# One written order for a kernel's opening: ten attention units, 32 weight pieces and 22 feed-forward steps

## The chip, the core and the metric

The kernel runs on one core of a Trainium2 chip. TensorE (PE) multiplies matrices, and its weight loads run beside its products; VectorE (DVE), ScalarE (ACT) and GpSimd (POOL) work element by element; SyncE (SP) here issues DMA transfers. Each engine takes its own instructions in their order and waits for the others by semaphores. The metric is the device time of one execution in microseconds (us); lower is better.

## The reference

Three stages follow each other: attention over a causal window of 64 keys, a dense feed-forward layer, and a layer of eight experts of which each token uses one. Reshapes and loops are cut.

```python
# q, k, v: (4, 8, 576, 64)
rel = pos[:, None] - pos[None, :]
mask = (rel >= 0) & (rel < 64)
scores = np.where(mask, np.matmul(q, k.T) / 8, -1e9)
attn = softmax(scores)
x = np.matmul(attn, v)                 # -> (2304 tokens, 512)

h = x @ w_in                           # (512, 2048)
g = np.where(h >= 1, h, np.where(h <= -1, 0, (h + 1) ** 2 / 4))
x = g @ w_out                          # (2048, 512) -> (2304, 512)

e = argmax(x @ w_gate)                 # 8 experts
out = gate_w * (np.maximum(x @ w1[e], 0) @ w2[e])
```

## The kernel before

All arithmetic is float32. A factor of a large product is held as a high part in the rounded format that TensorE takes (fp32r) and a low part, what the rounding left; a product is three passes (high with high, low with high, high with low).

**Units.** Attention is cut into 36 units: 128 tokens and four of the eight heads each. A unit (`unit_parts`) goes through: scores on PE with the mask added there (`u_qk`, L308 and L312), a maximum on VectorE (L351, L363), its scaled negative on ScalarE (L372), four exponentials on ScalarE (L382), a sum's reciprocal (L392, L393) and the scaling by it (L396, VectorE for units in `NORM_V`, else GpSimd), a transpose on PE (L420) and its copy on ScalarE (L423), the product with the values on PE (L438), and its split into high part (ScalarE, L450) and low part (VectorE, L452) in `xT`. The data of the first ten units (`qqr`, `vte`) lie in early buffers; units 10 and on load into one buffer for scores (`qk`, `RB = 1`) and one for values (`vt`, `VB = 1`), so that a load waits until the unit ahead has used its own.

**Weight pieces.** `w_in` and `w_out` arrive as doubles, in 16 pieces of 512 KB each (`wi`, `wo`, one for each f). Integer instructions turn a piece into float32 (`split_parts`): one on ScalarE (L193), three on VectorE (L206, L209, L213) or, for seven pieces (`SGN_P`), two on VectorE (L201, L209) beside one on GpSimd (L198); then the high part on ScalarE (L217) and the low part on GpSimd (L219). Two intermediate buffers `t` are shared by all pieces.

**Steps.** The dense layer takes the tokens in seven blocks (0 to 6) of 256 or 384 tokens (`BLOCKS`). A step is one block and one f: twelve matmuls (L482) into `h`, an activation (ScalarE L491, L492, VectorE L494, ScalarE L499 for the high part, L500 for the low part on VectorE or GpSimd by `GLO_P`), and the second layer (L519) into accumulators. `SEG` gives the order of blocks: before, block 0 does steps f = 0 to 7, then block 1 all 16, then block 0 the other eight, then blocks 2 to 6. A block's steps need the units of its tokens: units 0 to 3 for block 0, 4 to 9 for block 1, 10 to 13 for block 2. A second layer runs two steps behind its first.

**What sets the order.** `FIRST` lists the first 28 loads on SP. `HEAD` lists parts of units 0 to 3 and of weight pieces 0 to 4; `in_order` chains what these parts issue, engine by engine, as they are written. After that the units follow a plan of slots (`PLAN`, two slots to a step), the pieces follow due times (`wsplit`), and a scheduler at build time sets the order on PE, VectorE, ScalarE and GpSimd from the traced program. SP keeps the traced order up to step 8 (`SPN`); the loads of units 10 and on are traced between those of pieces.

Of the kernel before, what the change touches and what calls it, by code (L numbers as in the profile page):

```python
# [19 lines left out]
P = 128  # L20
# [14 lines left out]
RATE2 = 2  # L35
LA = 0
SPN = 8
SEG = [(0, 0, 8), (1, 0, 16), (0, 8, 16), (2, 0, 16), (3, 0, 16), (4, 0, 16), (5, 0, 16), (6, 0, 16)]
PLAN = {1: (-2, 16), 2: (36, 60), 3: (56, 84), 4: (86, 116), 5: (124, 150), 6: (154, 178)}
EARLY = 10  # L40
# [14 lines left out]
VB = 1  # L55
SGN_P = (10, 13, 16, 19, 20, 24, 30)
LEAD = (16, 0, 0)
ALT = 4
NQ = 15
MASK_PE = tuple(range(NQ))  # L60
GLO_P = (0, 1, 3, 4, 6, 7)
FIRST = "u0 m c u1 u2 v0 w u3 w v1 v2 w v3 w u4 u5 w v4 u6 v5 w u7 v6 u8 v7 u9 v8 v9".split()
DEPTH = 6, 3


HEAD = (
# [3 lines left out]
).split()  # L70
NORM_V = (0, 1, 2, 3, 12, 14, 32)
NORM_P = 14
# [3 lines left out]
KHI_V = (1, 4, 5, 7, 8, 9, 10, 15, 20, 26, 29, 30, 32, 34, 35)  # L76
PRO_A = 1
PRO_B = 6
WARM = 10
# [25 lines left out]
def mask_constants():  # L105

    r = np.arange(P)
    i = r[:, None] % 64
    ok = (r[None] >= i + 1) & (r[None] <= i + 64)
    new = ok & (r[None] >= 64)  # L110
    up = r[:, None] < 64
    m = np.stack([ok, np.where(up, new, ok), np.where(up, ok, new)], axis=1)
    return np.where(m, 0.0, NEG).astype(np.float32)


@with_exitstack
def kernel(
# [28 lines left out]
    ident = ct[:, C_ID:C_ID + P]  # L146
    mb = att.tile([P, 3, P], BF16, name="mb")
    ib = att.tile([P, P], BF16, name="ib")
    half = cp.tile([P, 1], F32, name="half")
# [23 lines left out]
    def load_w(kind, f):  # L173
        src = wi if kind == "i" else wo
        if f < KF - 2:
            raw = wp.tile([P, 512, 2], I32, tag="w", name="wraw")
        else:
            raw = sp.tile([P, 512, 2], I32, tag="st", name="sraw")
        nc.sync.dma_start(raw, src[:, f].bitcast(I32).rearrange("p (a b) -> p a b", b=2))
        return kind, f, raw  # L180

    def whole(gen):

        def run(*a):
            for _ in gen(*a):
                pass
        return run

    def split_parts(kind, f, raw):
        hw, lw = raw[:, :, 1], raw[:, :, 0]  # L190
        t = att.tile([P, 512], I32, tag="t", name="t", bufs=2)
        w = wp.tile([P, 2, 512], F32R, tag="w", name="w" + kind)
        nc.scalar.activation(t.bitcast(F32), hw.bitcast(F32), ACTF.Abs, scale=2.0**-112)  # L193
        yield
        onpool = 2 * f + (kind == "o") in SGN_P
        if onpool:

            nc.gpsimd.tensor_scalar(  # L198
                out=w[:, 1], in0=hw.bitcast(F32), scalar1=0.0, scalar2=None, op0=ALU.mult
            )  # L200
            nc.vector.scalar_tensor_tensor(  # L201
                out=t, in0=t, scalar=3, in1=w[:, 1].bitcast(I32), op0=ALU.logical_shift_left,
                op1=ALU.bitwise_or,
            )
        else:
            nc.vector.tensor_scalar(  # L206
                out=t, in0=t, scalar1=3, scalar2=None, op0=ALU.logical_shift_left
            )
# [3 lines left out]
        if not onpool:
            nc.vector.scalar_tensor_tensor(  # L213
                out=t, in0=hw, scalar=-0x80000000, in1=t, op0=ALU.bitwise_and, op1=ALU.bitwise_or
            )
        yield
        nc.scalar.activation(w[:, 0], t.bitcast(F32), ACTF.Copy)  # L217
        yield
        nc.gpsimd.tensor_tensor(  # L219
            out=w[:, 1], in0=t.bitcast(F32), in1=w[:, 0].bitcast(F32), op=ALU.subtract  # L220
        )
        (win if kind == "i" else wout)[f] = w

    split_w = whole(split_parts)

# [59 lines left out]
    def u_qk(u):  # L285
# [8 lines left out]
        if u < NQ:  # L294
# [5 lines left out]
            for pr in range(2):  # L300
# [4 lines left out]
                if pe:  # L305
                    for a, r, rows, o in outs:
                        m = 1 + a if kind == 1 + r else 0
                        nc.tensor.matmul(  # L308
                            o, ib[rows, 64 * a:64 * a + 64], mb[rows, m], start=True, stop=False
                        )  # L310
                for a, r, rows, o in outs:
                    nc.tensor.matmul(  # L312
# [175 lines left out]

    def act_g(h, n, pool):
        a = gp.tile([P, NG], F32, tag="a", name="a", bufs=2)  # L490
        nc.scalar.activation(a[:, :n], h[:, :n], ACTF.Relu, scale=0.5, bias=half[:, 0:1])  # L491
        nc.scalar.activation(a[:, :n], a[:, :n], ACTF.Square)  # L492

        nc.vector.scalar_tensor_tensor(  # L494
            out=a[:, :n], in0=h[:, :n], scalar=1.0, in1=a[:, :n], op0=ALU.max, op1=ALU.min
        )
        hi = gp.tile([P, NG], F32R, tag="ghi", name="ghi")
        lo = gp.tile([P, NG], F32R, tag="glo", name="glo")
        nc.scalar.activation(hi[:, :n], a[:, :n], ACTF.Copy)  # L499
        (nc.gpsimd if pool else nc.vector).tensor_tensor(  # L500
            out=lo[:, :n], in0=a[:, :n], in1=hi[:, :n].bitcast(F32), op=ALU.subtract
# [389 lines left out]
    for i, x in enumerate(FIRST):  # L891
        if x == "w":
            wload()
        elif x == "m":
            mt = sp.tile([P, 3, P], F32, tag="st", name="mt")
            nc.sync.dma_start(mt, msk)
            nc.vector.tensor_copy(mb, mt)
        elif x == "c":
            nc.sync.dma_start(ct, cst)
            nc.vector.tensor_copy(ib, ident)  # L900
        else:
# [11 lines left out]
    for j in range(NB2):  # L913
        for f in range(KF2):
            steps.append((2, j, f, f == 0, f == KF2 - 1, False))
    PRO = PRO_A * len(ub_[0]) + PRO_B
    base = PRO
    slots = {}
# [89 lines left out]
    f_at = {}
    for i, (ph, b, f, *_) in enumerate(steps):
        if ph == 1:  # L1010
            f_at.setdefault(f, i)

    def wsplit(s=None):

        if pend:
            kind, f = pend[0][:2]
            due = base + 2 * f_at[f] + (5 if kind == "o" else 0)
            if s is not None and due - s > LEAD[0] + LEAD[1] * f // 16:
                return
            split_w(*pend.pop(0))  # L1020
            if len(pend) < DEPTH[f >= 4]:
                wload()

    def run_slot(s):
# [6 lines left out]

    for _ in range(LA):
        wload()
    def in_order(traced):

        last = {}
        for i in traced:
# [6 lines left out]
            last[i.engine] = i  # L1044

    head = {}
    bb = nc.cur_bb.bb
    seen = {i.name for i in bb.instructions}
    for x in HEAD:
        k = int(x[-1])  # L1050
        key = x[:-1] in ("ab", "s", "hc", "wl"), k
        if key not in head:
            head[key] = split_parts(*pend.pop(0)) if key[0] else unit_parts(k)
        next(head[key], None)
    in_order([
        i for i in bb.instructions if i.name not in seen
        and i.engine in (mybir.EngineType.PE, mybir.EngineType.DVE, mybir.EngineType.Activation, mybir.EngineType.Pool)
    ])
    for _ in range(5):
        wload()  # L1060
    for s in range(PRO):
        run_slot(s)
    acc, g = {}, {}
    for i in range(len(steps) + 2):
        if i == SPN:
            sp_order.close()
        if i < len(steps):
            ph, b, f = steps[i][:3]
            if ph == 1:
                n = blocks[b][1]  # L1070
                while f not in win:
                    wsplit()
                g[i] = act_g(layer1(xT[b], win[f], n), n, i in GLO_P)
            else:
                g[i] = act_relu(layer1(xT2[b], W2["p"][0][f], NG), NG)
        run_slot(base + 2 * i)
        wsplit(base + 2 * i)
        if i >= 2:
            ph, b, f, first, last, partial = steps[i - 2]
            n = blocks[b][1] if ph == 1 else NG  # L1080
            if first:
                acc[ph, b] = accs(n)
            if ph == 1:
                while f not in wout:
                    wsplit()
                w = wout[f]
            else:
                w = W2["p"][1][f]
            layer2(acc[ph, b], g.pop(i - 2), w, first, last)
            if last:  # L1090
                if ph == 1:
                    evac1(b, acc.pop((ph, b)), partial)
                else:
                    evac2(b, acc.pop((ph, b)))
        run_slot(base + 2 * i + 1)
        if i == len(steps) - 1 + LEFT[0]:
            L["h"] = left1(L["w"], L["xl"])
        if i == len(steps) - 1 + LEFT[1]:
            L["g"] = left_turn(L["h"])
        if LEAD[2]:  # L1100
            wsplit(base + 2 * i + 1)

# [71 lines left out]
```

## Time and profile before

| | us |
|---|---|
| median of three runs | 756.37 (756.35 to 757.07) |
| the profiled execution, whole | 757.15 |
| its span, first to last instruction | 755.4 |

| engine | busy us | share of the span |
|---|---|---|
| PE | 719.0 | 95% |
| VectorE | 496.0 | 66% |
| ScalarE | 419.0 | 55% |
| GpSimd | 207.8 | 28% |

The busy time is that of an engine with at least one instruction in work. A view by stretches gives, for windows of the span, the busy time of each engine, the clock granted to TensorE (1.00 is 2.4 GHz, 0.50 is 1.2 GHz), the DMA engines' share and the rate of transfers. A timeline lists instructions with their start and duration and, in brackets, how long the engine had been idle and for whom. On VectorE a following instruction can start a little before the one ahead has ended, so that the distance of two starts is what an instruction takes of the engine. Lines in brackets above are lines of the kernel before.

### The profile page before, as it was taken

The page shows a single profiled execution, that of the slowest core. Times are in us where ns is not written, and L with a number is a line of the kernel's source. Part 1 is how long each engine was busy: PE and PEld are TensorE (multiplying, and loading weights), DVE is VectorE, ACT ScalarE, POOL GpSimd, SP SyncE. Part 2 cuts the span into 40 slices and gives each one's busy share as a digit, 9 for nine tenths or more (in the row PEclk, how much of TensorE's full clock was granted, in tenths as well). Part 3 has the DMA queues.
Part 4 walks back from the last instruction along what each step waited for, and adds up shares of the span by engine and source line. Part 5 has one row for each costly group of instructions (what it writes and reads, how often), then busy time and mean ns, then how long its engine had stood idle before and what let it go on. Part 6 is the DMA issues. An engine that isn't in the chain of part 4 may idle for free. (4 is left out here: it accounts for less than half of the span.)

```text
span 755.4 us, 12426 instructions
## 1 busy us (share of the span) xinstructions
PE 719.0 (95%) x4507; PEld 631.3 (84%) x4507; DVE 496.0 (66%) x1053; ACT 419.0 (55%) x1031; POOL 207.8 (28%) x162
## 2 busy tenths in 40 slices
PE   6597799999999999999999999999999999999996
PEld 3475689888898999888988899987888999888985
DVE  5998988535758655776687334887779989752110
ACT  5777765575757775865586534466443325163212
POOL 0467744202412211330320000366220202065100
PEclk8799899999999999999999999999999999999999
DMA  9940630223432421535254321443334233053101
GB/s 330 402 163 19 208 138 29 57 84 112 154 99 84 143 96 58 173 91 127 62 176 90 83 85 67 123 131 106 117 71 119 49 105 85 23 152 125 44 1 53
DMA packets 66690, 83.77 MB, mean 111 GB/s; under 512 B 35671, under 2 KB 41559, under 8 KB 66498
## 3 DMA queue, kind: packets, MB, share of 16 engines
q1 hardware_dynamic: 66466, 82.52, 35.5%
q8 instruction: 36, 0.59, 0.3%
q0 software_dynamic: 160, 0.43, 0.2%
q14 instruction: 28, 0.23, 0.1%
HBM read 60.74 MB, written 14.42 MB: 100 GB/s over the span
## 5 line engine op out<-in xcount | busy, mean ns | idle before, releaser
L482 PE MATMUL h<-xT,wi 128*128 128x384 f32 (+1 forms) x1344 | 233.4, 321 | 7.4 <-ACT xT L450 3.8
L482 PEld LDWEIGHTS h<-xT,wi 128*128 128x128 f32 x1344 | 212.2, 192 | 20.6 <-DVE a L494 5.4
L519 PE MATMUL acc<-wo,ghi 128*128 128x512 f32 x576 | 155.5, 397 | 0.7 <-ACT wo L217 0.7
L519 PEld LDWEIGHTS acc<-wo,ghi 128*128 128x128 f32 x576 | 103.2, 188 | 16.5 <-ACT wo L217 1.1
L614 DVE CUSTOM_DVE_ANT_0 junk<-xg,wgb 128x512 bf16<-128x512 f32 x144 | 113.8, 790 | 3.2
L482 PE MATMUL h<-xT,we 128*128 128x384 f32 x576 | 110.6, 338 | 3.6 <-DVE glo L509 3.6
L482 PEld LDWEIGHTS h<-xT,we 128*128 128x128 f32 x576 | 101.8, 188 | 9.6 <-DVE glo L509 5.3
L494 DVE SCALAR_TENSOR_TENSOR a<-h,a 128x384 f32<-128x384 f32 (+1 forms) x112 | 55.5, 496 | 63.8 <-ACT a L492 63.2
L500 DVE TENSOR_TENSOR glo<-a,ghi 128x384 fp32r<-128x384 f32 (+1 forms) x106 | 71.4, 674 | 37.7 <-ACT ghi L499 37.6
L519 PE MATMUL acc<-wo,glo 128*128 128x512 f32 x288 | 85.3, 394 | 0.2
L491 ACT ACTIVATE a<-h,half 128x384 f32<-128x384 f32 (+1 forms) x112 | 58.7, 525 | 43.8 <-PE h L482 41.9
L519 PE MATMUL acc<-we,ghi 128*128 128x512 f32 x288 | 78.4, 394 | 0.0
L499 ACT ACTIVATE ghi<-a 128x384 fp32r<-128x384 f32 (+1 forms) x112 | 53.0, 474 | 38.7 <-DVE a L494 38.4
L519 PEld LDWEIGHTS acc<-wo,glo 128*128 128x128 f32 x288 | 53.6, 188 | 13.1 <-POOL glo L500 1.1
L508 ACT ACTIVATE ghi<-h 128x384 fp32r<-128x384 f32 x48 | 23.1, 481 | 71.2 <-PE h L482 62.4
L509 DVE SCALAR_TENSOR_TENSOR glo<-h,ghi 128x384 fp32r<-128x384 f32 x48 | 26.6, 555 | 52.7 <-ACT ghi L508 52.7
L519 PEld LDWEIGHTS acc<-we,ghi 128*128 128x128 f32 x288 | 53.0, 188 | 8.2
L959 POOL TENSOR_TENSOR xT<-xj,xT 128x256 fp32r<-128x256 f32 x36 | 31.4, 883 | 90.4 <-ACT xT L958 90.4
L492 ACT ACTIVATE a<-a 128x384 f32<-128x384 f32 (+1 forms) x112 | 53.1, 475 | 2.3
L282 POOL TENSOR_TENSOR qs<-qk,qs 128x768 fp32r<-128x768 f32 x18 | 34.7, 1926 | 68.0 <-DVE qs L274 27.7
L279 POOL TENSOR_TENSOR qs<-qk,qs 64x512 fp32r<-64x512 f32 x16 | 22.0, 1377 | 109.7 <-ACT qs L272 82.5
L688 POOL TENSOR_TENSOR we<-er,we 128x512 fp32r<-128x512 f32 x16 | 23.9, 1499 | 99.4 <-DMA er<-in_w_dram 87.2
(169 smaller groups left out, 940.6 us busy)
## 6 DMA issues: line engine op xcount, KB each, us to landing
qk<-in_qk_dram SPq DMA_DIRECT2D x21, 640.0 KB, 3.9
er<-in_w_dram SPq DMA_DIRECT2D x32, 256.0 KB, 2.8
wraw<-in_wi_dram SPq DMA_DIRECT2D x14, 512.0 KB, 7.5
wraw<-in_wo_dram SPq DMA_DIRECT2D x14, 512.0 KB, 6.9
vt<-in_vv_dram SPq DMA_DIRECT2D x26, 256.0 KB, 2.8
xg<-x2s SPq DMA_DIRECT2D x18, 256.0 KB, 2.7
out_dram<-y SPq DMA_DIRECT2D x18, 256.0 KB, 2.1
qqr<-in_qq_dram SPq DMA_DIRECT2D x10, 320.0 KB, 7.2
```

The costliest lines, as they stand in the source:

```text
L282: keng.tensor_tensor(out=k, in0=raw[:, 512:], in1=kh.bitcast(F32), op=ALU.subtract)
L482: nc.tensor.matmul(h[:, :n], w[:, wa, k * P:k * P + P], x[:, xa, k, :n], start=(i == 0), stop=(i == 3 * KD - 1),)
L491: nc.scalar.activation(a[:, :n], h[:, :n], ACTF.Relu, scale=0.5, bias=half[:, 0:1])
L492: nc.scalar.activation(a[:, :n], a[:, :n], ACTF.Square)
L494: nc.vector.scalar_tensor_tensor(out=a[:, :n], in0=h[:, :n], scalar=1.0, in1=a[:, :n], op0=ALU.max, op1=ALU.min)
L499: nc.scalar.activation(hi[:, :n], a[:, :n], ACTF.Copy)
L500: (nc.gpsimd if pool else nc.vector).tensor_tensor(out=lo[:, :n], in0=a[:, :n], in1=hi[:, :n].bitcast(F32), op=ALU.subtract)
L509: nc.vector.scalar_tensor_tensor(out=lo[:, :n], in0=h[:, :n], scalar=0.0, in1=hi[:, :n].bitcast(F32), op0=ALU.max, op1=ALU.subtract,)
L519: nc.tensor.matmul(a, ga[:, t * P:t * P + P], w[:, wa], start=(first and j == 0), stop=(last and j == 2),)
L614: tc.keep_in_program_order(nc.vector.tensor_tensor_reduce(out=junk, in0=xg[t], in1=Z["wgb"][:, e], scale=1.0, scalar=0.0, op0=ALU.mult, op ...
L688: nc.gpsimd.tensor_tensor(out=w[:, 1], in0=raw, in1=w[:, 0].bitcast(F32), op=ALU.subtract)
L959: (nc.vector if 2 * t + i in PL_V else nc.gpsimd).tensor_tensor(out=lo, in0=r, in1=hi.bitcast(F32), op=ALU.subtract)
```

## The change

The opening is written out whole. `HEAD` now lists 369 parts: the ten units 0 to 9, all 32 weight pieces, and the parts of 22 steps (`ga` first layer, `rl` the two activations, `st`, `gh`, `gl`, `gb` second layer, `ev` a block's evacuation), and `in_order` chains all that they issue. The steps' function is cut into parts for this (`act_parts`, `step_parts`). Block 0 does six steps first instead of eight. Each piece's part `s` issues the next piece's load, eight pieces ahead; SP keeps the traced order to the end of the chain, and the loads of unit 10 alone are traced inside it.

All 32 low parts of the weights move from GpSimd (L219) to VectorE (L223 of the changed kernel), and the seven pieces of `SGN_P` go the way of the others. Scalings of units 4, 6 and 8 move to VectorE; the low parts of the six steps of block 0 are on GpSimd. The mask and the small identity come from the host as one array in bf16, so two casts go. The last four pieces load into buffers `qs` of the attention instead of the evacuation's. `PLAN` has no entry for block 1, and block 2's units 10 to 13 stand in slots 46 to 58 instead of 36 to 60; `base`, from which slots count, is 0 instead of 10, that is, they lie as far from their steps as before but for this entry.

```diff
-SEG = [(0, 0, 8), (1, 0, 16), (0, 8, 16), (2, 0, 16), (3, 0, 16), (4, 0, 16), (5, 0, 16), (6, 0, 16)]
-PLAN = {1: (-2, 16), 2: (36, 60), 3: (56, 84), 4: (86, 116), 5: (124, 150), 6: (154, 178)}
+SEG = [(0, 0, 6), (1, 0, 16), (0, 6, 16), (2, 0, 16), (3, 0, 16), (4, 0, 16), (5, 0, 16), (6, 0, 16)]
+PLAN = {2: (46, 58), 3: (56, 84), 4: (86, 116), 5: (124, 150), 6: (154, 178)}
...
-GLO_P = (0, 1, 3, 4, 6, 7)
+GLO_P = tuple(range(6))
...
+    "wl17 rl10 s18 ab19 gb7 rl11 st10 s19 hc18 ga12 gh10 st11 hc19 gl10 wl18 wl19 ga13 ab20 rl12 "
...
-NORM_V = (0, 1, 2, 3, 12, 14, 32)
+NORM_V = (0, 1, 2, 3, 4, 6, 8, 12, 14, 32)
...
-            raw = sp.tile([P, 512, 2], I32, tag="st", name="sraw")
+            raw = att.tile([P, 512, 2], I32, tag="qs", name="sraw", bufs=QB)
...
-        onpool = 2 * f + (kind == "o") in SGN_P
-        if onpool:
...
-        nc.gpsimd.tensor_tensor(
+        nc.vector.tensor_tensor(
             out=w[:, 1], in0=t.bitcast(F32), in1=w[:, 0].bitcast(F32), op=ALU.subtract
         )
...
-            mt = sp.tile([P, 3, P], F32, tag="st", name="mt")
-            nc.sync.dma_start(mt, msk)
-            nc.vector.tensor_copy(mb, mt)
+            nc.sync.dma_start(cb.bitcast(U16), msk)
...
+    def step_parts(i):
+        _, b, f = steps[i][:3]
+        n = blocks[b][1]
+        g[i] = yield from act_parts(xT[b], win[f], n, i in GLO_P)
+        yield
+        second(i)
+        yield
+        evac(i)
+        yield
...
         next(head[key], None)
+        if name == "s":
+            wload()
+        if x == "av9":
+            u_load(10)
+            v_load(10)
...
+    sp_order.close()
+    done = 1 + max(int(x[2:]) for x in HEAD if x[:2] == "ga")
+    for i in range(done, len(steps) + 2):
```

SP, the loads before, from the middle of the weight pieces on (`qk` and `vt` are loads of units 10 and on, `wraw` a weight piece):

```order
L254 DMA vt_989<-in_vv_dram 128x512
L179 DMA wraw_999<-in_wi_dram 128x1024
L179 DMA wraw_1037<-in_wo_dram 128x1024
L243 DMA qk_1389<-in_qq_dram 128x640
L243 DMA qk_1563<-in_qq_dram 128x640
L179 DMA wraw_1074<-in_wi_dram 128x1024
L243 DMA qk_1734<-in_qq_dram 128x640
L179 DMA wraw_1114<-in_wo_dram 128x1024
```

SP now, the end of the weight pieces (`sraw` are the last four):

```order
L191 DMA wraw_1135<-in_wo_dram 128x1024
L191 DMA sraw_1156<-in_wi_dram 128x1024
L191 DMA wraw_1202<-in_wo_dram 128x1024
L191 DMA sraw_1221<-in_wi_dram 128x1024
L191 DMA sraw_1265<-in_wo_dram 128x1024
L191 DMA sraw_1288<-in_wo_dram 128x1024
L245 DMA qk_1615<-in_qq_dram 128x640
L575 DMA x2s_78<-xrow_1680 128x2x512
```

The loads of units 11 and on have moved behind the last piece; unit 10's stand ten loads before this cut.

VectorE before, in steps of block 1 (`t` is a piece's intermediate, `a` and `glo` belong to steps):

```order
L201 SCALAR_TENSOR_TENSOR t<-t,wo 128x512
L500 TENSOR_TENSOR glo<-a,ghi 128x384
L209 SCALAR_TENSOR_TENSOR t<-wraw,t 128x512
L206 TENSOR_SCALAR t<-t 128x512
L494 SCALAR_TENSOR_TENSOR a<-h,a 128x384
L209 SCALAR_TENSOR_TENSOR t<-wraw,t 128x512
L500 TENSOR_TENSOR glo<-a,ghi 128x384
L213 SCALAR_TENSOR_TENSOR t<-wraw,t 128x512
```

VectorE now, in steps of block 1:

```order
L509 TENSOR_TENSOR glo<-a,ghi 128x384
L223 TENSOR_TENSOR wo<-t,wo 128x512
L223 TENSOR_TENSOR wi<-t,wi 128x512
L211 TENSOR_SCALAR t<-t 128x512
L214 SCALAR_TENSOR_TENSOR t<-wraw,t 128x512
L217 SCALAR_TENSOR_TENSOR t<-wraw,t 128x512
L501 SCALAR_TENSOR_TENSOR a<-h,a 128x384
L211 TENSOR_SCALAR t<-t 128x512
L214 SCALAR_TENSOR_TENSOR t<-wraw,t 128x512
L217 SCALAR_TENSOR_TENSOR t<-wraw,t 128x512
```

A pair of pieces has six instructions ahead of its low parts, and the two low parts (L223) have come into VectorE's queue.

GpSimd before, from the first weight piece:

```order
L219 TENSOR_TENSOR wi<-t,wi 128x512 x2
L219 TENSOR_TENSOR wo<-t,wo 128x512
L396 TENSOR_TENSOR sr<-sr,rc 128x512
L219 TENSOR_TENSOR wi<-t,wi 128x512
L219 TENSOR_TENSOR wo<-t,wo 128x512
L396 TENSOR_TENSOR sr<-sr,rc 128x512
```

GpSimd now, all that it has in the chain, and three scalings of units 10 and on behind it:

```order
L400 TENSOR_TENSOR sr<-sr,rc 128x512
L509 TENSOR_TENSOR glo<-a,ghi 128x256 x2
L400 TENSOR_TENSOR sr<-sr,rc 128x512
L509 TENSOR_TENSOR glo<-a,ghi 128x256 x2
L400 TENSOR_TENSOR sr<-sr,rc 128x512
L509 TENSOR_TENSOR glo<-a,ghi 128x256 x2
L400 TENSOR_TENSOR sr<-sr,rc 128x512 x3
```

Nine instructions are left there of some fifty before.

## Rows read from the trace of the kernel before

**Rows 1.** Busy time by stretches; each row: length, each engine's busy us (instructions).
```profile
core 0: us, PE busy (x) PEld busy (x) DVE busy (x) ACT busy (x) POOL busy (x), PEclk, DMA share, GB/s
0.00:10.00 10.00, 5.89 (x82) 2.90 (x82) 2.44 (x8) 3.06 (x11) 0.18 (x4) 1.00 0.79 265
10.00:60.00 50.00, 38.04 (x393) 30.27 (x386) 46.60 (x73) 36.82 (x117) 25.95 (x20) 0.83 0.76 285
60.00:80.00 20.00, 16.01 (x164) 11.88 (x164) 16.62 (x29) 15.41 (x53) 14.40 (x11) 0.91 0.14 42
...
100.00:130.00 30.00, 30.00 (x153) 26.71 (x152) 25.91 (x36) 19.51 (x37) 15.17 (x11) 1.00 0.15 47
89.60:96.40 6.80, 5.18 (x27) 5.07 (x28) 5.92 (x10) 5.95 (x18) 4.98 (x4) 0.50 0.55 167
```

**Rows 2.** SP's own waits, 0 to 160 us: total us, times, longest us.
```profile
SPq L243 <- PE S L312: 36.7, 4, 19.2
```

**Rows 3.** Timeline of PE: start us, duration us, instruction, [idle before].
```profile
43.72 0.60 PE L420 MATMUL pt<-ct,sr 128*128 128x128 f32 x4
...
47.07 0.25 PE L308 MATMUL S<-mb,ib 64*64 64x128 bf16 x4
...
47.74 0.97 PE L438 MATMUL av<-pb,vte 128*64 128x64 f32 x16
...
49.01 1.70 PE L482 MATMUL h<-xT,wi 128*128 128x256 f32 x12
...
52.11 0.74 PE L482 MATMUL h<-xT,wi 128*128 128x256 f32 x4
...
103.75 2.27 PE L482 MATMUL h<-xT,wi 128*128 128x384 f32 x12
...
150.96 2.27 PE L482 MATMUL h<-xT,wi 128*128 128x384 f32 x12
...
155.15 1.59 PE L482 MATMUL h<-xT,wi 128*128 128x256 f32 x12
...
186.61 1.60 PE L482 MATMUL h<-xT,wi 128*128 128x256 f32 x12
```

**Rows 4.** Timeline of VectorE, 11 to 20 us, in the same columns.
```profile
11.75 0.43 DVE L206 TENSOR_SCALAR t<-t 128x512 int32<-128x512 int32 x1 [0.83 <-ACT t L193]
12.21 0.69 DVE L209 SCALAR_TENSOR_TENSOR t<-wraw,t 128x512 int32<-128x512 int32 x1
12.93 0.69 DVE L213 SCALAR_TENSOR_TENSOR t<-wraw,t 128x512 int32<-128x512 int32 x1
13.54 0.68 DVE L351 TENSOR_REDUCE mx<-S 128x4 f32<-128x512 f32 x1
14.14 0.16 DVE L392 TENSOR_SCALAR rc<-sm 128x4 f32<-128x4 f32 x1
...
14.55 0.69 DVE L396 TENSOR_TENSOR sr<-sr,rc 128x512 f32<-128x512 f32 x1
15.16 1.50 DVE L206 TENSOR_SCALAR t<-t 128x512 int32<-128x512 int32 x1
...
18.96 1.72 DVE L396 TENSOR_TENSOR sr<-sr,rc 128x512 f32<-128x512 f32 x1
```

**Rows 5.** Timeline of GpSimd in the same stretch.
```profile
14.74 1.63 POOL L219 TENSOR_TENSOR wi<-t,wi 128x512 fp32r<-128x512 f32 x1 [14.30 <-ACT nm L372]
18.85 1.28 POOL L219 TENSOR_TENSOR wi<-t,wi 128x512 fp32r<-128x512 f32 x1 [2.48 <-ACT wi L217]
```

**Rows 6.** VectorE by line and shape, 0 to 120 us: busy us, mean ns | idle before.
```profile
L209 DVE SCALAR_TENSOR_TENSOR t<-wraw,t 128x512 int32<-128x512 int32 x27 | 25.1, 928 | 0.6
L213 DVE SCALAR_TENSOR_TENSOR t<-wraw,t 128x512 int32<-128x512 int32 x21 | 18.6, 887 | 0.5
L206 DVE TENSOR_SCALAR t<-t 128x512 int32<-128x512 int32 x21 | 15.4, 735 | 2.1 <-ACT t L193 2.1
```

**Rows 7.** DMA issues, 0 to 150 us: count, KB each, median us from issue to landing.
```profile
qk<-in_qq_dram SPq DMA_DIRECT2D x5, 320.0 KB, 3.1
```

More of the change, by code (lines that the diff above doesn't have):

```diff
@@ L35 @@
 RATE2 = 2
-LA = 0
-SPN = 8
-SEG = [(0, 0, 8), (1, 0, 16), (0, 8, 16), (2, 0, 16), (3, 0, 16), (4, 0, 16), (5, 0, 16), (6, 0, 16)]
-PLAN = {1: (-2, 16), 2: (36, 60), 3: (56, 84), 4: (86, 116), 5: (124, 150), 6: (154, 178)}
+SEG = [(0, 0, 6), (1, 0, 16), (0, 6, 16), (2, 0, 16), (3, 0, 16), (4, 0, 16), (5, 0, 16), (6, 0, 16)]
+PLAN = {2: (46, 58), 3: (56, 84), 4: (86, 116), 5: (124, 150), 6: (154, 178)}
 EARLY = 10
@@ L55 @@
 VB = 1
-SGN_P = (10, 13, 16, 19, 20, 24, 30)
-LEAD = (16, 0, 0)
 ALT = 4
@@ L60 @@
 MASK_PE = tuple(range(NQ))
-GLO_P = (0, 1, 3, 4, 6, 7)
-FIRST = "u0 m c u1 u2 v0 w u3 w v1 v2 w v3 w u4 u5 w v4 u6 v5 w u7 v6 u8 v7 u9 v8 v9".split()
-DEPTH = 6, 3
+GLO_P = tuple(range(6))
+FIRST = "u0 m u1 c u2 w v0 u3 w v1 w v2 w v3 u4 w v4 u5 w v5 u6 w v6 u7 w v7 u8 v8 u9 v9".split()
+BEHIND = 10
 HEAD = (
[3 rows of a table removed]
[18 rows of a table added]
 ).split()
-NORM_V = (0, 1, 2, 3, 12, 14, 32)
+NORM_V = (0, 1, 2, 3, 4, 6, 8, 12, 14, 32)
 NORM_P = 14
@@ L76 @@
 KHI_V = (1, 4, 5, 7, 8, 9, 10, 15, 20, 26, 29, 30, 32, 34, 35)
-PRO_A = 1
-PRO_B = 6
 WARM = 10
@@ L112, in mask_constants @@
     m = np.stack([ok, np.where(up, new, ok), np.where(up, ok, new)], axis=1)
-    return np.where(m, 0.0, NEG).astype(np.float32)
+    m = np.concatenate([np.where(m, 0.0, NEG), np.eye(P)[:, None]], axis=1).astype(np.float32)
+    return ((m.view(np.uint32) + 0x8000) >> 16).astype(np.uint16)
 @with_exitstack
@@ L146 @@
     ident = ct[:, C_ID:C_ID + P]
-    mb = att.tile([P, 3, P], BF16, name="mb")
-    ib = att.tile([P, P], BF16, name="ib")
+    cb = att.tile([P, 4, P], BF16, name="cb")
+    mb, ib = cb[:, :3], cb[:, 3]
     half = cp.tile([P, 1], F32, name="half")
@@ L184, in run @@
         def run(*a):
-            for _ in gen(*a):
-                pass
+            parts = gen(*a)
+            while True:
+                try:
+                    next(parts)
+                except StopIteration as e:
+                    return e.value
         return run
@@ L194, in split_parts @@
         yield
-        onpool = 2 * f + (kind == "o") in SGN_P
-        if onpool:
[L198 to L208, printed above, removed]
+        nc.vector.tensor_scalar(
+            out=t, in0=t, scalar1=3, scalar2=None, op0=ALU.logical_shift_left
+        )
         nc.vector.scalar_tensor_tensor(
@@ L211, in split_parts @@
         )
[L212 to L215, printed above, removed]
+        nc.vector.scalar_tensor_tensor(
+            out=t, in0=hw, scalar=-0x80000000, in1=t, op0=ALU.bitwise_and, op1=ALU.bitwise_or
+        )
         yield
@@ L222, in split_parts @@
         (win if kind == "i" else wout)[f] = w
-    split_w = whole(split_parts)
     units = [
@@ L307, in u_qk @@
                         m = 1 + a if kind == 1 + r else 0
-                        nc.tensor.matmul(
+                        mm = nc.tensor.matmul(
                             o, ib[rows, 64 * a:64 * a + 64], mb[rows, m], start=True, stop=False
                         )
+                        if u == BEHIND:
+                            tc.keep_in_program_order(mm)
                 for a, r, rows, o in outs:
@@ L487, in layer1, with act_parts @@
         return h
-    def act_g(h, n, pool):
+    def act_parts(x, w, n, pool):
+        h = layer1(x, w, n)
+        yield
         a = gp.tile([P, NG], F32, tag="a", name="a", bufs=2)
@@ L499, in act_g @@
         nc.scalar.activation(hi[:, :n], a[:, :n], ACTF.Copy)
+        yield
         (nc.gpsimd if pool else nc.vector).tensor_tensor(
@@ L894 @@
         elif x == "m":
-            mt = sp.tile([P, 3, P], F32, tag="st", name="mt")
-            nc.sync.dma_start(mt, msk)
-            nc.vector.tensor_copy(mb, mt)
+            nc.sync.dma_start(cb.bitcast(U16), msk)
         elif x == "c":
             nc.sync.dma_start(ct, cst)
-            nc.vector.tensor_copy(ib, ident)
         else:
@@ L915 @@
             steps.append((2, j, f, f == 0, f == KF2 - 1, False))
-    PRO = PRO_A * len(ub_[0]) + PRO_B
-    base = PRO
+    base = 0
     slots = {}
@@ L1007 @@
                 at(s0 + PREP[2] + PREP[3] * i + PI * m, prep, j * TB + i, m)
[L1008 to L1022, printed above, removed]
     def run_slot(s):
@@ L1030, in run_slot @@
                 v_load(a[0] + VB)
-    for _ in range(LA):
-        wload()
     def in_order(traced):
@@ L1044, in in_order, with second, evac @@
             last[i.engine] = i
+    acc, g = {}, {}
+    def second(i):
+        ph, b, f, first, last, _ = steps[i]
+        if first:
+            acc[ph, b] = accs(blocks[b][1] if ph == 1 else NG)
+        layer2(acc[ph, b], g.pop(i), wout[f] if ph == 1 else W2["p"][1][f], first, last)
+    def evac(i):
+        ph, b, _, _, last, partial = steps[i]
+        if last and ph == 1:
+            evac1(b, acc.pop((ph, b)), partial)
+        elif last:
+            evac2(b, acc.pop((ph, b)))
+    def step_parts(i):
+        _, b, f = steps[i][:3]
+        n = blocks[b][1]
+        g[i] = yield from act_parts(xT[b], win[f], n, i in GLO_P)
+        yield
+        second(i)
+        yield
+        evac(i)
+        yield
     head = {}
@@ L1049 @@
     for x in HEAD:
-        k = int(x[-1])
-        key = x[:-1] in ("ab", "s", "hc", "wl"), k
+        name = x.rstrip("0123456789")
+        k = int(x[len(name):])
+        key = "w" if name in ("ab", "s", "hc", "wl") else "g" if name[0] == "g" or name in ("rl", "st", "ev") else "u", k
         if key not in head:
-            head[key] = split_parts(*pend.pop(0)) if key[0] else unit_parts(k)
+            head[key] = (
+                split_parts(*pend.pop(0)) if key[0] == "w" else step_parts(k) if key[0] == "g" else unit_parts(k)
+            )
         next(head[key], None)
+        if name == "s":
[3 more added lines that the diff above has]
+            v_load(10)
     in_order([
@@ L1058 @@
     ])
[L1059 to L1066, printed above, removed]
+    sp_order.close()
+    done = 1 + max(int(x[2:]) for x in HEAD if x[:2] == "ga")
+    for i in range(done, len(steps) + 2):
         if i < len(steps):
@@ L1070 @@
                 n = blocks[b][1]
-                while f not in win:
-                    wsplit()
-                g[i] = act_g(layer1(xT[b], win[f], n), n, i in GLO_P)
+                g[i] = whole(act_parts)(xT[b], win[f], n, i in GLO_P)
             else:
@@ L1076 @@
         run_slot(base + 2 * i)
-        wsplit(base + 2 * i)
         if i >= 2:
[L1079 to L1094, printed above, removed]
+            second(i - 2)
+            evac(i - 2)
         run_slot(base + 2 * i + 1)
@@ L1099 @@
             L["g"] = left_turn(L["h"])
-        if LEAD[2]:
-            wsplit(base + 2 * i + 1)
     left_out(left2(L["w"], L["g"]), L["idx"], L["s"])
```

20 rows, old and new, of the table HEAD are left out of this document.

## The prediction

> **What bounds the kernel now.** I read the busy times by stretches first, then the timeline of PE, then what VectorE does while PE waits. From 100 to 130 us PE is busy for all of 30 us; before that it is not: 38.04 of 50 us from 10 to 60, 16.01 of 20 from 60 to 80 [rows 1]. Its clock is granted at 0.83 and 0.91 there, against 1.00 from 100 on, and from 89.6 to 96.4 it is at half, 1.2 GHz, all the time [rows 1]. So the end is set by how early PE comes to be full, and what keeps it from that is VectorE: 46.60 of 50 us busy from 10 to 60, a pace of 0.93, with ScalarE at 36.82 [rows 1]. From 60 to 80 VectorE falls to 16.62 of 20 and the DMA engines to a share of 0.14 [rows 1]: SP stands 36.7 us at loads of units 10 and on, which wait for a buffer that PE still reads, and weight pieces are queued behind them [rows 2].
>
> **A mark to measure against.** Before, the first step of block 0's second part (f = 8) starts on PE at 155.15 and the first of block 2 at 186.61 [rows 3]. Afterwards that second part starts at f = 6, two steps earlier in the work, and with ten units done where eleven were. A step of 256 columns takes 52.11 - 49.01 = 3.1 us [rows 3]; a unit on PE 0.67 for scores (47.07 to 47.74), 0.97 for values, 0.60 for transposes, 2.2 in all [rows 3]. Were nothing gained, the second part would start at 155.15 - 6.2 - 2.2 = 146.7. What it starts earlier than that is the gain, if the rest is as it was.
>
> **VectorE's work in the chain.** By the distances of starts where GpSimd is idle [rows 4]: a piece's three instructions take 0.46 + 0.72 + 0.61 = 1.79, a maximum 0.60, a reciprocal's two 0.41, a scaling of 512 columns 0.61. The low part of a piece is a subtraction of the same size as that scaling, so 0.61; at 384 columns I estimate 0.47 by its ratio, at 256 0.34. So the sum: 32 pieces x (1.79 + 0.61) = 76.8; ten units x (0.60 + 0.41 + 0.34) = 13.5 and seven scalings 4.3; six short steps 2.0, sixteen long ones x 2 x 0.47 = 15.0; one evacuation 0.6. That is 112.2. Up to the low part of unit 9, which block 1 waits for, the chain has 13 pieces with all four instructions (31.2), all units (17.8) and six short steps (2.0): 51.0. Up to the low part of step 18, which the second-last second layer of the chain waits for, all but 2.9: 109.3.
>
> **GpSimd beside it.** A subtraction of GpSimd's costs VectorE time: a scaling of 0.69 takes 1.72 beside the 1.28 at 18.85, an instruction of 0.43 takes 1.50 beside the 1.63 at 14.74 [rows 4, 5]. In the chain nine shorter ones are left, all ahead of block 1; I put each at 0.7, between 0 (hidden in a wait) and the 1.07 just seen: 6.3 in all.
>
> The Trainium skill ("Perfetto Trace Analysis", Optimizing Scalar/DVE Operations) says that with a saturated VectorE it may make sense to offload to GpSimd, which speaks against this move: 19.5 us more for VectorE. The same section adds that the two share a read port, so that it might not help; the rows agree with this half, 1.03 us lost for 0.61 saved.
>
> **The sum.** By 10 us VectorE was busy 2.44 us [rows 1], of which I take it to do chain work all the time now, since the two casts at the start go and the mask load ahead of the first scores is smaller: 2.4. From there I let it keep its pace of 0.93. Unit 9 is ready at 10 + (51.0 + 6.3 - 2.4) / 0.93 = 69.0. From then on PE has 16 first layers, 14 long second layers and two short ones. A long step takes (150.96 - 103.75) / 11 = 4.29 [rows 3]; two first layers alone are 4.2, two short second layers 3.1; so 14 x 4.29 + 7.3 = 67.4, and the mark comes at 136.4 by PE. By VectorE, step 18's low part is there at 10 + (109.3 + 6.3 - 2.4) / 0.93 = 131.7, and two second layers of 2.15 follow: 136.0. The two engines are nearly even, so small waits of one are not made good by the other. PE has holes up to block 1, and with holes it was granted 0.83; one stretch of 6.8 us at half clock [rows 1] that reaches into block 1 would cost it 3.4, of which I count 2, as VectorE has its own queue to work off meanwhile. The mark: 138.
>
> Transfers don't bound this: by 60 us 0.265 x 10 + 0.285 x 50 = 16.9 MB had come [rows 1], and the chain up to block 1 needs ten units with their values (5.9 MB), 15 pieces (7.9) and constants (0.3). Weight loads no longer stand behind those of unit 11 and on. ScalarE gets no instruction more, and has a quarter of its time free [rows 1]. The casts, the mask array and the other buffer for four pieces I cost at nothing: they are ahead of the first scores, or between pieces that VectorE has not reached; uncovered, the last piece, whose buffer comes free late, waits for one load, about 3 us [rows 7].
>
> **Behind the chain.** Ten steps and four units are left up to block 2; before, 31.46 us held eight and three [rows 3]; by the prices above the rest cancels. But units 10 to 13 now stand in 12 slots instead of 24, with one buffer for scores. A load takes 3.1 us [rows 7], a step with a unit 5.3, so it is mostly covered; I charge 1.5, between 0 and 4. Gain: 146.7 - 138 - 1.5 = 7.2. The span goes from 755.4 to 748.2. The profiled execution took 757.15, 1.75 beyond its span, and lies 0.8 above the median of 756.37: 748.2 + 1.75 - 0.8 = **749**.
>
> **Rivals.** (1) The written order holds VectorE up: an engine may take no later instruction while its next waits, where the scheduler had interleaved; with GpSimd's delays gone, waits that these covered come out as idle time. The place is a pair of pieces: the next one's first ScalarE instruction needs a buffer `t` that the last low part frees. The point of decision is a pace of 113.2 / (146.7 - 1.5 - 4.3 - 10) = 0.865; 25.91 of 30 from 100 to 130 is just that [rows 1], though VectorE wasn't pressed there. At 0.82 step 18 is ready at 148 and the mark at 152.3: 5.6 and 1.5 lost, 763.5. For it: the two engines' even load. Against: 0.93 over 50 us, half of it under the old written order.
> (2) VectorE at 0.97, with the clock kept: unit 9 at 66.6, the mark at 134, nothing behind: 12.7 gained, 743.6.
> (3) Loads of units 11 to 13 uncovered: each leaves PE without a unit for up to 3 us, and block 2 starts 9 later instead of 1.5: no change, 756.5. For it: SP's waits at just these buffers [rows 2].
> (4) VectorE's long instructions are not GpSimd's doing. Then the means stay at 0.93, 0.89 and 0.74 [rows 6] against 0.69, 0.69 and 0.43 [rows 4]: 0.75 a piece, 24 over the chain, 26 at the pace: 775. Rows 4 and 5 lie side by side, which speaks against it. This is also what the Trainium skill's first half, taken alone, would give.
>
> **How the numbers follow.** Forecast 0.56, (1) 0.14, (2) 0.18, (3) 0.08, (4) 0.04. For the forecast's own bounds, 0.86 to 0.97 for the pace, 0 to 3.4 for the clock and 0 to 4 behind give 743 to 759. From 742 to 759 the range holds the forecast, (3), most of (2) and the edge of (1), some 0.82. A measurement can tell about 0.2%, 1.5 us, from no change. Faster: the forecast and (2), 0.74; same: (3), 0.08; slower: (1) and (4), 0.18.
>
> **What would show it.** In the changed kernel's trace: VectorE's three piece instructions at 0.43, 0.69 and 0.69 from block 1 on, its busy share near 0.93 from 10 to 130; block 1's first matmul of 384 columns near 69 us, the second part of block 0 at 138, block 2 near 179; SP without a wait for scores before the last piece. The prediction is wrong if block 1 starts after 75, if VectorE waits for ScalarE by more than a tenth of its time, or if PE stands still between 138 and 180 for unit loads.

## The result, and the profile after

| | before | after |
|---|---|---|
| median, us | 756.72 (4 runs) | 746.49 (744.77 to 747.34, 4 runs) |
| ratio, 95% interval | | 0.986 (0.9839 to 0.9881) |
| profiled execution's span | 755.4 | 743.0 |
| PE, busy us | 719.0 | 714.0 |
| GpSimd, busy us | 207.8 | 144.5 |

The median falls by 10.2 us, the profiled span, which belongs to the shortest of the four executions, by 12.4. The forecast was 749.

The stretches of the changed kernel answer to [rows 1], in the same columns (busy us of PE, PEld, DVE, ACT, POOL, then the clock):

```profile
10.00:60.00 50.00, 39.31 (x444) 32.40 (x443) 45.62 (x94) 40.55 (x134) 8.72 (x9) 0.86 0.91 346
60.00:80.00 20.00, 18.40 (x98) 16.83 (x99) 18.51 (x35) 14.24 (x27) 0.00 (x0) 0.84 0.42 132
80.00:100.00 20.00, 20.00 (x104) 18.43 (x104) 19.35 (x36) 14.62 (x28) 0.00 (x0) 1.00 0.01 1
...
64.20:130.00 65.80, 65.80 (x328) 59.88 (x328) 61.25 (x110) 47.45 (x88) 0.00 (x0) 0.98 0.16 49
130.00:170.00 40.00, 40.00 (x377) 34.42 (x377) 15.40 (x41) 26.71 (x87) 3.54 (x4) 1.00 0.34 110
170.00:200.00 30.00, 28.09 (x218) 25.16 (x217) 17.77 (x34) 18.45 (x52) 12.57 (x8) 1.00 0.40 128
```

PE is busy in every instant from 64.2 to 170, where before it came to that only near 100. VectorE is as busy from 10 to 60 as it was, 45.62 against 46.60, but it does 94 instructions in that time where it did 73; 11 of the 94 are low parts that came over. A hole has opened on PE from 170 to 200.

The timeline of PE (start, duration, instruction) answers to [rows 3]: the first step of block 1, of block 0's second part (f = 6) and its third step (f = 8), of block 2, and a step inside block 4:

```profile
64.22 5.48 PE L486 MATMUL h<-xT,wi 128*128 128x384 f32 x24
...
130.04 1.24 PE L486 MATMUL h<-xT,wi 128*128 128x256 f32 x9
...
138.63 1.11 PE L486 MATMUL h<-xT,wi 128*128 128x256 f32 x8
...
169.69 0.39 PE L486 MATMUL h<-xT,wi 128*128 128x256 f32 x2
...
330.10 2.09 PE L486 MATMUL h<-xT,wi 128*128 128x384 f32 x11
```

The last of these steps started before at:

```profile
341.34 1.92 PE L482 MATMUL h<-xT,wi 128*128 128x384 f32 x10
```

At f = 8 of block 0, with the same 24 first layers behind it, the changed kernel is 155.15 - 138.63 = 16.5 us ahead; at block 2 186.61 - 169.69 = 16.9; inside block 4 only 341.34 - 330.10 = 11.2. Part of the lead is given back on the way.

VectorE's groups by line and shape, 0 to 130 us (busy us, mean ns | idle before), answer to [rows 6]; L223 are the low parts that came over:

```profile
L214 DVE SCALAR_TENSOR_TENSOR t<-wraw,t 128x512 int32<-128x512 int32 x28 | 20.5, 733 | 1.0
L217 DVE SCALAR_TENSOR_TENSOR t<-wraw,t 128x512 int32<-128x512 int32 x28 | 19.4, 692 | 1.0
L211 DVE TENSOR_SCALAR t<-t 128x512 int32<-128x512 int32 x32 | 14.2, 444 | 1.9 <-ACT t L209 1.7
L223 DVE TENSOR_TENSOR wi<-t,wi 128x512 fp32r<-128x512 f32 x16 | 11.5, 718 | 0.1
```

The three piece instructions fell from 928, 887 and 735 ns to 733, 692 and 444, that is by 0.68 us a piece in all; the new low part takes 0.7.

### The profile page after: what moved, and what is told of

Same layout as the page of the kernel before. It is cut to its first block, busy times and chain, and to the rows that moved or that the text cites. A ratio compares the mean times of both kernels' runs of the same rounds, so it can differ in the third digit from the quotient of the medians.

```text
span 743.0 us, 12418 instructions
## 1 busy us (share of the span) xinstructions
PE 714.0 (96%) x4507; PEld 630.6 (85%) x4507; DVE 488.7 (66%) x1093; ACT 418.2 (56%) x1031; POOL 144.5 (19%) x120
## 5 line engine op out<-in xcount | busy, mean ns | idle before, releaser
L486 PE MATMUL h<-xT,wi 128*128 128x384 f32 (+1 forms) x1344 | 230.4, 319 | 3.3 <-DVE a L501 3.1
L501 DVE SCALAR_TENSOR_TENSOR a<-h,a 128x384 f32<-128x384 f32 (+1 forms) x112 | 55.5, 497 | 66.8 <-ACT a L498 66.0
L509 DVE TENSOR_TENSOR glo<-a,ghi 128x384 fp32r<-128x384 f32 (+1 forms) x106 | 60.4, 571 | 36.4 <-ACT ghi L507 36.3
L528 PEld LDWEIGHTS acc<-wo,glo 128*128 128x128 f32 x288 | 53.5, 188 | 11.9 <-issue 0.2
L528 PE MATMUL acc<-we,glo 128*128 128x512 f32 x144 | 44.1, 395 | 0.0
```

The costliest lines, as they stand in the source:

```text
L486: nc.tensor.matmul(h[:, :n], w[:, wa, k * P:k * P + P], x[:, xa, k, :n], start=(i == 0), stop=(i == 3 * KD - 1),)
L501: nc.vector.scalar_tensor_tensor(out=a[:, :n], in0=h[:, :n], scalar=1.0, in1=a[:, :n], op0=ALU.max, op1=ALU.min)
L509: (nc.gpsimd if pool else nc.vector).tensor_tensor(out=lo[:, :n], in0=a[:, :n], in1=hi[:, :n].bitcast(F32), op=ALU.subtract)
L528: nc.tensor.matmul(a, ga[:, t * P:t * P + P], w[:, wa], start=(first and j == 0), stop=(last and j == 2),)
```

## The experiments

Two theories stood against each other. One: the written order fills PE early, and moving the low parts costs VectorE about what it gives back. The other: GpSimd's subtractions hold VectorE up, and taking them out is the gain, whatever the order. The prediction had not said which of the two edits brings how much. A third suspect was SP's queue. Times are medians beside the kernel before on the same chip; ratios carry their 95% interval. Executions of one kernel differ by up to 0.7% (e8: 740.21 to 745.4), so differences of 2 us between experiments that did not run side by side are not leaned on.

### e1 and e12: the kernel before, low parts on VectorE

```diff
-SGN_P = (10, 13, 16, 19, 20, 24, 30)
+SGN_P = ()
...
-        nc.gpsimd.tensor_tensor(
+        nc.vector.tensor_tensor(
             out=w[:, 1], in0=t.bitcast(F32), in1=w[:, 0].bitcast(F32), op=ALU.subtract
         )
```

> The kernel before with all 32 low parts of the weights on VectorE and no piece of SGN_P on GpSimd; order and loads as before. If the gain is the one written order, PE's holes up to 100 us stay, and the time is 752 to 759 (VectorE does 32 x 0.6 more and loses as much less beside GpSimd). If GpSimd's interference was what held the opening up, most of the gain is here already: 749 or less.

Measured: 744.69 against 756.63, 0.9848 (0.9828 to 0.9869). The second theory's case, and all of the gain, with the old plan of slots, the eight steps and the old list of loads. The order itself isn't the old one: the chain ends with unit 3 here, and behind it the scheduler, at build time, set the order anew for a VectorE that has the low parts. On PE the two traces have the same sequence only for the first 248 matmuls, up to 35.6 us of the kernel before. So e1 shows the move together with what the scheduler makes of it; what the low parts cost in one fixed order is for e2 and e6 to show. Its stretches:

```profile
10.00:60.00 50.00, 41.92 (x444) 34.70 (x444) 46.98 (x96) 41.12 (x135) 10.50 (x9) 0.83 0.67 261
60.00:80.00 20.00, 17.82 (x154) 13.96 (x152) 18.12 (x35) 15.91 (x51) 5.20 (x5) 0.91 0.50 184
80.00:100.00 20.00, 20.00 (x134) 17.33 (x134) 19.36 (x39) 15.57 (x36) 0.00 (x0) 1.00 0.58 196
```

VectorE is busy 46.98 us from 10 to 60, as before [rows 1], and does 96 instructions in it instead of 73, 13 of them low parts. PE is full from 80 on. And what is won stays: the step f = 8 of block 0 and the step inside block 4 start at

```profile
142.40 1.36 PE L482 MATMUL h<-xT,wi 128*128 128x256 f32 x10
...
328.56 1.75 PE L482 MATMUL h<-xT,wi 128*128 128x384 f32 x9
```

155.15 - 142.40 = 12.75 us early, and 341.34 - 328.56 = 12.78.

> The kernel of e1 again, beside the changed kernel on the same chip: 743.5 to 746.5. If the written order of the changed kernel does make a gain that units 10 to 13 give back behind it, this is 0 to 2 us faster than e11.

Measured beside the changed kernel: 745.96 against 756.73, 0.9854 (0.984 to 0.9867).

### e11: the changed kernel on the same chip as e12

> The changed kernel as it is, beside the others on the same chip: 745 to 747.5. If the chain is worth nothing beyond taking GpSimd out, within 2 us of e12.

Measured: 744.81, 0.9853 (0.983 to 0.9876). No difference to e12 that these runs, with intervals of some 2 us to either side, can tell: the written order, the six steps and the loads' order have together no visible worth beyond what e12 has.

### e2: the changed kernel, low parts on GpSimd

```diff
-        nc.vector.tensor_tensor(
+        nc.gpsimd.tensor_tensor(
             out=w[:, 1], in0=t.bitcast(F32), in1=w[:, 0].bitcast(F32), op=ALU.subtract
         )
```

> The changed kernel with the 32 low parts back on GpSimd, at the same places of the written order. If order makes the gain, VectorE is relieved of 19.5 us and loses 0.6 to 1.0 beside each GpSimd subtraction, and PE, which was full from 64 us on, loses 0 to 4: 746 to 751. If taking GpSimd out makes it, the first step of block 1 comes after 72 us instead of 64, PE has holes behind it, and the time is 753 or more.

Measured: 755.8 against 756.63, 0.9989 (0.9976 to 1.0003). The gain is gone, though the sequence on PE and on ScalarE is the changed kernel's. Its stretches:

```profile
60.00:80.00 20.00, 15.47 (x82) 13.54 (x82) 17.18 (x26) 11.99 (x23) 7.18 (x6) 0.83 0.41 132
80.00:100.00 20.00, 18.94 (x94) 16.66 (x94) 17.88 (x26) 12.53 (x25) 7.87 (x6) 1.00 0.00 0
100.00:130.00 30.00, 26.27 (x126) 22.24 (x126) 25.65 (x37) 18.18 (x35) 10.35 (x8) 1.00 0.10 24
```

PE has holes until 130 now, later than it had in the kernel before. From 60 to 100 VectorE does 52 instructions where the changed kernel did 71 (35 + 36); 14 of the 71 are low parts, which e2 has on GpSimd, so that 57 stand against 52. In one point the expectation failed: block 1 started at 65.59, not after 72. Nearly all of the loss comes behind that.

### e5 and e6: the interference by itself

e5 moves the chain's last nine GpSimd instructions to VectorE as well; e6 adds to it 32 subtractions on GpSimd that nothing waits for.

```diff
-GLO_P = tuple(range(6))
+GLO_P = ()
...
-NORM_V = (0, 1, 2, 3, 4, 6, 8, 12, 14, 32)
+NORM_V = (0, 1, 2, 3, 4, 5, 6, 7, 8, 9, 12, 14, 32)
```

```diff
+        if "j" not in junk:
+            junk["j"] = sp.tile([P, 2, 512], F32, tag="st", name="spare")
+        nc.gpsimd.tensor_tensor(
+            out=junk["j"][:, 0], in0=w[:, 0].bitcast(F32), in1=w[:, 0].bitcast(F32), op=ALU.subtract
+        )
```

> The changed kernel with the last nine GpSimd instructions of the chain (three scalings, six low parts of block 0's steps) on VectorE too. If GpSimd's subtractions cost VectorE what they take off it, nothing is lost or gained: 744 to 748. If VectorE's load is the limit ahead of block 1, 9 x 0.4 to 0.6 us come on top: 748 to 751.

Measured: 743.58 against 756.04, 0.9841 (0.9823 to 0.986): nine instructions more on VectorE, and no slower.

> The kernel of e5 with 32 subtractions on GpSimd, one beside each weight piece, of the size of the old low parts, which read the finished high part and write a spare tile that nobody reads; VectorE still does the real ones, so no instruction waits for GpSimd. They are work beyond the reference's and change no output. If GpSimd slows VectorE by being in the same memory port, VectorE loses 0.6 to 1.0 beside each: 19 to 32 us over the chain, and the time goes to 757 to 775. If it was the late low parts that hurt (GpSimd's longer instruction and queue, ScalarE waiting for buffers), nobody waits here and the time stays within 2 us of e5.

Measured: 760.45, 0.5 to 0.8% above the kernel before (1.0058, 1.0041 to 1.0075), 16.9 us above e5. No result of these subtractions is read, and in the trace no engine waits for one; the sequence on PE, ScalarE and VectorE is that of e5. So GpSimd's mere work slows the opening, not the lateness of its results. VectorE and GpSimd side by side in e6, in two timelines; L229 is a real low part on VectorE, L226 a subtraction into the spare tile:

```profile
60.71 1.22 DVE L229 TENSOR_TENSOR wo<-t,wo 128x512 fp32r<-128x512 f32 x1
...
65.24 0.69 DVE L215 SCALAR_TENSOR_TENSOR t<-wraw,t 128x512 int32<-128x512 int32 x1
65.97 1.41 DVE L218 SCALAR_TENSOR_TENSOR t<-wraw,t 128x512 int32<-128x512 int32 x1
67.30 0.68 DVE L229 TENSOR_TENSOR wo<-t,wo 128x512 fp32r<-128x512 f32 x1
```

```profile
60.34 1.04 POOL L226 TENSOR_TENSOR spare<-wo 128x512 f32<-128x512 f32 x1 [6.16 <-ACT wo L222]
65.35 1.48 POOL L226 TENSOR_TENSOR spare<-wo 128x512 f32<-128x512 f32 x1 [3.97 <-ACT wo L222]
```

The two instructions that began while a GpSimd one ran take 1.22 and 1.41. The one that had begun just ahead of it, at 65.24, takes 0.69, and the next low part, with GpSimd idle, 0.68.

### e7: only the low parts moved

e1 with `SGN_P` as it was.

> The kernel before with the 32 low parts on VectorE, while the seven pieces of SGN_P keep their GpSimd instruction. If every GpSimd instruction of this size costs alike, 32 of 39 are gone, and about 32/39 of 12 us are gained: 745.5 to 748. If the seven, of 1.5 to 2.0 us with VectorE waiting for their result, were the worse ones, 749 to 754.

Measured: 747.05 against 756.04, 0.989 (0.9866 to 0.9915). Most of the gain is the 32 low parts; the seven sign instructions are what is left to e1, some 2 to 3 us, though the two intervals overlap.

### e4: units 10 and 11 loaded early

The kernel before with units 10 and 11 in early buffers:

```diff
-EARLY = 10
+EARLY = 12
...
-FIRST = "... v8 v9".split()
+FIRST = "... v8 v9 u10 v10 u11 v11".split()
```

> The kernel before with the data of units 10 and 11 in early buffers, so that SP no longer stands at unit 11's load with weight pieces behind it. If that wait starved the opening, VectorE's busy share from 60 to 80 us rises from 0.83 above 0.93, PE is full before 90 us, and the time is 748 to 752. If it only hid other waits, 754 to 758.

Measured: 756.87 against 756.63, 0.9998 (0.9985 to 1.0011). Its stretches:

```profile
10.00:60.00 50.00, 39.04 (x394) 30.83 (x386) 47.13 (x74) 36.46 (x117) 26.12 (x20) 0.83 0.82 303
60.00:80.00 20.00, 16.23 (x172) 12.36 (x173) 16.59 (x28) 15.69 (x57) 15.05 (x12) 0.91 0.12 36
```

VectorE's 16.59 of 20 us from 60 to 80 is the 16.62 of [rows 1]. But the edit moved SP's wait more than it took it away: SP now stands at unit 12's load. Its waits from 0 to 160 us in e4, and then in e1, in the columns of [rows 2]:

```profile
SPq L243 <- PE S L312: 31.7, 2, 17.3
```

```profile
SPq L243 <- PE S L312: 39.2, 4, 23.1
```

So the time of e4 alone doesn't clear this suspect. Two other things do: e1 has all of the gain with a longer wait of this kind, and in the kernel before, until the last four pieces (from 119.9 us on, with PE full), the engines waited for a weight piece's load only once:

```profile
ACT t L193 <- DMA wraw<-in_wi_dram: 0.9, 1, 0.9
```

### e3: the changed kernel without the chain

The call of `in_order` is left out; the trace order stays.

> The changed kernel, traced in the same written order, but without the chain: the scheduler may reorder on PE, VectorE, ScalarE and GpSimd. If the chain itself is needed, most of the gain goes: 752 to 758. If the traced order, the six steps and the loads' order already make it, the time stays at 745 to 748.

Measured: 761.81 against 756.63, 1.0057 (1.0036 to 1.0077), slower than either case expected. The stretches:

```profile
60.00:80.00 20.00, 14.05 (x102) 11.43 (x94) 19.61 (x38) 14.13 (x33) 2.15 (x2) 0.66 0.45 148
80.00:100.00 20.00, 13.99 (x62) 12.89 (x61) 19.43 (x38) 13.54 (x26) 0.00 (x0) 0.83 0.01 1
```

VectorE is full, yet PE is not, and PE's clock is granted at 0.66 and 0.83; PE's longest wait from 60 to 100, 6.0 us, is for VectorE's part of an activation (L501). So VectorE doesn't do first what PE needs first. With this traced order the chain is needed, by 15 us; the kernel before, with its own plan and the low parts moved, comes to the same time without it (e12).

### e8, e9 and e10: how far it goes

e8 puts the first half of unit 10 into the chain and loads unit 11 behind its scores.

```diff
-"... ga21 gh18 s31 hc30 gb16 wl30 hc31 gl18 wl31 gb17 rl20 gh19 ..."
+"... ga21 gh18 s31 hc30 gb16 qk10 wl30 hc31 gl18 wl31 mx10 gb17 rl20 nm10 gh19 ..."
...
+        if x == "qk10":
+            u_load(11)
```

> The changed kernel with unit 10's scores, maximum, exponentials and scaling in the chain, among its last steps, and units 11 to 13 in the slots as before, with unit 11's load issued behind unit 10's scores. If PE's 1.9 us of holes from 170 to 200 us come from units 10 to 13 being late, most of them go: 743.5 to 745.5. If they come from the order behind, no change: 745.5 to 748. If the unit's work pushes VectorE's last pieces back, 748 to 750.

Measured: 742.88 against 756.04, 0.983 (0.9795 to 0.9865). PE's hole from 170 to 200 is gone:

```profile
170.00:200.00 30.00, 30.00 (x228) 26.78 (x228) 20.73 (x41) 21.28 (x62) 12.20 (x8) 1.00 0.43 149
```

The time's interval still covers that of the changed kernel, so the trace shows the hole's cause and its size, 1.9 us, and the times don't confirm a price.

e9 is e1 with the scalings of units 4 to 9 and block 0's low parts on VectorE too (two scalings, of units 10 and 11, stayed on GpSimd).

> The kernel before, its order and loads kept, with no GpSimd instruction at all in the opening: weights' low parts, SGN_P's, scalings of units 4 to 9 and low parts of block 0's steps on VectorE. If GpSimd's interference is the whole cause, this is as fast as the changed kernel without GpSimd (743.6) and 1 to 4 faster than e1: 741 to 745. If the written order adds something of its own, 745 to 748.

Measured: 742.36 against 756.73, 0.9811 (0.9798 to 0.9825), the lowest median here, though e8's interval covers it; again with the old plan and an order by the scheduler. On the same chip it is 3.6 us below e12, with intervals apart: the other GpSimd instructions of the opening cost time too.

> The changed kernel with both: unit 10's first half in the chain (e8) and the last nine GpSimd instructions of the chain on VectorE (e5). If the two gains are separate (3 at most each), 739 to 742. If unit 10 in the chain needs the VectorE time that e5 takes, 742 to 745.

Measured: 744.7, 0.984 (0.9827 to 0.9854). Neither small gain was clear of the noise by itself, and together they are no more; why is open. With hardly a GpSimd instruction in either opening, the written order, with unit 10 in it, is not faster than the scheduler's of e9 on the same chip but 2.3 us slower, with intervals that just miss each other.

## Why the prediction was right in its number, and what its reason left out

**What bounds the kernel.** That PE waits in the opening, that VectorE is what it waits for, and that an early full PE carries to the end: right (e1 keeps 12.75 us from 142 to the step in block 4). That weight loads behind SP's wait were part of it: wrong (e1 has the gain with that wait, and only 0.9 us was lost to a load up to the last four pieces).

**The low parts.** What is missing is in the paragraph on them. I read the right rows, 1.03 us lost beside one GpSimd subtraction for 0.61 saved. VectorE's work in the sum is priced by rows with GpSimd idle, so the end of the interference is in it, and rival (4) even says what its staying would cost, 24 us over the chain. But the sum was made for the changed kernel's absolute time and could not tell one edit from the other, and I never priced the low parts alone. By the same rows that would have been 32 x (1.03 - 0.61) = 13.4 us, an estimate; e7 measured 9.0 for them and e1 11.9 with the seven sign instructions. The move is the whole gain (e1, e12), and without it the written order has none (e2). Rival (4) is refuted from both sides, by e6 and by the means of the piece instructions. The Trainium skill ("Perfetto Trace Analysis", Optimizing Scalar/DVE Operations) says that with a saturated VectorE offloading to GpSimd may make sense, and that it might not help, since the two share a read port. The measurements of this case are on the side of the second half: taking work back from GpSimd gained those 9.0 to 11.9 us.

**Its sizes.** Step by step, against the changed kernel's trace:
- Unit 9 ready at 69.0: block 1 started at 64.2, and unit 9's low part followed at 65.2. VectorE's pace, 0.93, was nearly right: 45.62 of 50 (0.91) and 61.25 of 65.8 (0.93). The term that was too large is the nine GpSimd instructions, 6.3 us: the means of 733, 444 and 718 ns stand 0.04, 0.02 and 0.03 above what e5 has without GpSimd or what L217 has, some 2.5 us over the pieces.
- Block 1 in 67.4 by PE and 2 more for the clock: it took 130.04 - 64.22 = 65.8 at a clock of 0.98. My 4.29 us a step was a mean over a stretch that held four score matmuls and a wait of 0.26 too; an undisturbed step there takes 4.19 (116.88 to 121.07).
- The mark at 138 came at 130.0. But its comparison, 146.7, was wrong as well: I took one unit's work as the difference. Before, scores of units 11 to 13 had been done ahead of the mark too. By the groups of PE by line behind it, 80 score matmuls are left after (64 at f = 8), 16 before; a unit has 16 and takes 0.67, so three units' scores (2.0) and the rest of unit 10 (0.35 and 0.90 by the distances of starts, 1.3) were merely postponed at f = 8: of the 16.5 us there 16.5 - 2.0 - 1.3 = 13.2 were gained.
- Behind the chain 1.5: PE lost 30 - 28.09 = 1.9 from 170 to 200, and 13.2 - 1.9 = 11.3 is the 11.2 found inside block 4. This was sized well, and e8 shows that units 10 to 13 are its cause.

Two errors of size partly cancelled: the mark was put 8 us too late (138 for 130.0), which took gain away, and its comparison was 16.7 - 13.2 = 3.5 us too generous (146.7 - 130.0 = 16.7), which gave some back. That 749 lies within 2.5 us of the median is in part luck.

**The rivals.** (1) did not happen: VectorE's pace in the written order stayed at 0.91 to 0.93, above the 0.865 at which it begins. (2) came nearer to the times, 66.6 and 134 against 64.2 and 130.0, but not by its reason: VectorE had less to do than the sum said, and its pace did not rise. (3) happened in small, 1.9 of its 9.

## What to carry to other kernels

Where VectorE is near full, the work that GpSimd takes from it must be priced by what VectorE loses beside it: read a VectorE instruction's duration with and without a GpSimd instruction next to it. Here 32 subtractions that were "off" the bound engine cost some 9 us (e7, e2), and 32 that nothing waits for were enough to cost 17. When several edits come together, forecast each one alone: the smallest edit here, one word, carried most of the gain (e7).

## What the runs showed of the hardware

In these traces a VectorE instruction with its inputs in SBUF and a GpSimd one don't share the time side by side: the one that begins second waits. In e6, 25 VectorE instructions of 512 columns with two inputs in SBUF began while GpSimd's subtraction ran, and each ended 0.54 to 0.55 us behind its end, however much of it was left. Two of them are in the rows of e6, 61.93 against 61.38 and 67.38 against 66.83, and one in the kernel before, 20.68 against 20.13 [rows 4, 5]. The 17 that had begun ahead of one kept their 0.68 to 0.69, and it was GpSimd's that grew: 1.48 at 65.35, begun 0.11 behind VectorE's, against 1.04 at 60.34. So what VectorE loses there is the rest of GpSimd's instruction, less some 0.14 us.

The loss is not even over VectorE's instructions. SBUF and PSUM are the two on-chip memories that the kernel places its tiles in; scores (`S`) and a step's `h` are in PSUM. Over 0 to 120 us before, the piece instructions with inputs in SBUF stood at 928, 887 and 735 ns [rows 6] against 0.69, 0.69 and 0.43 alone [rows 4], while those that read PSUM kept their time. Two groups of the kernel before over 0 to 160 us, in the columns of [rows 6], the first with one input in PSUM (`h`), the second a maximum over PSUM:

```profile
L494 DVE SCALAR_TENSOR_TENSOR a<-h,a 128x384 f32<-128x384 f32 x16 | 8.8, 553 | 4.5 <-ACT a L492 4.5
L351 DVE TENSOR_REDUCE mx<-S 128x4 f32<-128x512 f32 x12 | 8.1, 677 | 0.9 <-PE S L312 0.9
```

In e5, with no GpSimd instruction in the chain, their like take 0.553 and 0.686. Seven of these L494 and seven of these maxima overlapped a GpSimd instruction, and none took more than 0.560 and 0.684; of the 16 L500 of the same size, with two inputs in SBUF, the ten that overlapped none took at most 0.559, the six others up to 1.573. The Trainium skill ("GPSIMD Engine Reference", 8. Key points) says that GpSimd contends with VectorE instructions that have two inputs in SBUF or run in a two-port performance mode. The trace agrees for the two kinds with two SBUF inputs and for those with a PSUM input; whether the third, with one SBUF input, ran in such a mode no run here shows.
